# Issuing the V rows of a fused attention and MoE kernel from GpSimd instead of SyncE

## The chip, the cores and the metric

One Trainium2 chip, one core of it. The metric is the device time of one execution in microseconds (us). Engines are named as in the profile: PE (TensorE matmuls), PEld (its weight loads), DVE (VectorE), ACT (ScalarE), POOL (GpSimd), SP (SyncE, which here only issues transfers). Sixteen DMA engines serve all queues. Transfers issued by SP run on the hardware queue that the profile calls q1, transfers issued by POOL on the software queue q0, and the few that ACT issues on q10.

## The reference

Two layers, one after the other. Attention over q, k, v of shape (8, 8, 576, 64), that is 8 batches of 8 heads, is the sum of two parts: a coarse one on means of 4 positions, and a local one with a band mask. Its output, as 4608 tokens of 512, goes through a two-layer block without bias.

```python
def _attn_ref(q, k, v):
    ...                              # Sd = S // 4, scale = 1/sqrt(D)
    q_d = q.reshape(B, H, Sd, 4, D).mean(axis=3)        # k_d, v_d alike
    out_up = np.repeat(sm_attn(q_d, k_d, v_d), 4, axis=2)
    mask = np.abs(pos[:, None] - pos[None, :]) < 4
    scores = np.where(mask, scale * q @ k.T, -1e9)
    return out_up + softmax(scores) @ v

def _moe_ref(x, w_in, w_out):        # (4608, 512), (512, 2048), (2048, 512)
    h = x @ w_in
    return (h - np.tanh(h)) @ w_out
```

## The kernel before

Heads are handled in pairs: 32 pairs, four to a batch, a batch being a block `kb` of the dense part. For each pair `p` the kernel loads K and Q (`load_qk`, lines 363 to 369, two transfers of 256 KB into the staging tile `st`, 4 buffers) and V (`load_v`, lines 384 to 393, one transfer of 160 KB per head into `vst`, 5 buffers, so pair p+5 uses the buffer of pair p). A V transfer consists of 640 rows of 256 bytes: 128 partitions times 5 overlapping row tiles. `prep_v` (line 423) casts `vst` to bf16 as `vw` (line 427) on whichever of POOL, ACT and DVE the order names, and thereby sets the `vst` buffer free. From pair 12 on, V is also loaded a second time in groups of four positions (`load_v4`, lines 395 to 403, tile `v4`, shown as `v`), which POOL sums for the coarse part (lines 440 and 444); for earlier pairs PE makes these sums from `vw` (`pool_v`, line 458). Some of the `load_v4` transfers are issued by POOL (list `SOFT`), the others by SP.

For a pair, `attention` casts K and Q to bf16 (`qr`, line 502), turns them (PE transposes at line 510 for pairs 0 to 11, DMA transposes on SP after that), pools them (`half`, `qkd`, lines 593 to 627), makes the scores (lines 657 to 671), the exponentials on ACT (lines 676 to 684), the band mask (line 711), and the product with V (line 725). The result, divided by its sums (line 742), is turned again and joined into `xT` (line 760), the input of the dense part.

The dense part has, for each block, `mm1` (line 803: x times w_in, tanh on ACT at 814, subtraction on DVE at 817, giving `gT`) and `mm2` (line 883: `gT` times w_out). Blocks 5 to 7 use a seven-product scheme instead of `mm2` (line 1030), which needs sums of `gT` (`token_sums`, line 965). Rows left over from the 512-token tiles go through `left1` and `left2` (lines 829 and 855). While PE has nothing of the real work in the first microseconds, it runs filler matmuls (line 1240).

The weights are loaded by POOL, w_in and w_out in four transfers of 512 KB each (`load_w`, lines 405 to 421). Before the first of each, POOL copies one element of a named staging buffer (`GATE`, `OGATE`, line 416), so that the weights' transfers start only after that buffer has landed.

The order is not left to a scheduler. Class `Plan` collects all operations with planned costs, a list of alternatives (which engine), priorities and earliest starting times (`REL`), and lays them out engine by engine; the kernel then issues each engine's instructions in that fixed order. `GIVEN` names, letter by letter, which engine takes each free choice. `ONE` says for which pairs the two score steps are put as one, `WIDE` whether a `token_sums` step is one instruction or two halves. Every engine runs its instructions strictly in this order, and a waiting instruction holds up all that stands behind it on its engine. SP is such an engine too: a K, Q or output transfer stands behind a V transfer that waits for its `vst` buffer.

Of the kernel before, what the change touches and what calls it, by code (L numbers as in the profile page):

```python
# [14 lines left out]
class Plan:  # L15
# [17 lines left out]
    def op(self, eng, ns, fn, reads=(), writes=(), pri=0, after=0.0, slack=0.0,  # L33
           port=False, opens=None, uses=(), choice=None, rows=128, share=0.4):
        i = len(self.ops)
        deps = set()
        for key in reads:
            if key in self.last_write:
                deps.add(self.last_write[key])
        for key in writes:  # L40
            if key in self.last_write:
                deps.add(self.last_write[key])
            deps.update(self.readers.get(key, ()))
        for key in reads:
            self.readers.setdefault(key, set()).add(i)
        for key in writes:
            self.last_write[key] = i
            self.readers[key] = set()
        deps.discard(i)
        names = set(uses)  # L50
        if opens and not isinstance(opens, list):
            opens = [opens]
        for o in opens or ():
            names.add(o[0])
        for n in names:
            self.users.setdefault(n, []).append(i)
        if choice:

            letter = self.given[self.choices]
            self.choices += 1  # L60
            named = [a[:4] for a in choice if a[0][0] == letter]
            choice = named or [a for a in choice if len(a) == 4]
        alts = {a[0]: a for a in choice} if choice else {eng: (eng, ns, fn, port)}
        self.ops.append(dict(alts=alts, deps=deps, pri=pri, after=after, slack=slack,
                             opens=opens, names=names, rows=rows, share=share,
                             what=(list(writes) + [None])[0]))
        return i
# [135 lines left out]
def kernel(  # L203
# [9 lines left out]
    nc = tc.nc  # L213
    B, H, S, D = q.shape
# [5 lines left out]
    SCALE = 1.0 / float(D) ** 0.5  # L220
    N_FF = Dff // 128
    N_DC = Dm // 128
    WIDE = [c == "1" for c in "1011"]
    NBLK, NR, LEFT = B, 3, S - 512
    STEP = 112
    NT = 5
# [12 lines left out]


    KIN = [c == "1" for c in "11111111111100000000000000000000"]
    HALF = [c == "1" for c in "00001000000000000000000000000000"]

    SOFT = [c == "1" for c in "00001110011000110010001001000001"]
    VIN = [c == "1" for c in "11111111111100000000000000000000"]
    BACK = [c == "1" for c in "11111111111100000000000000000000"]
    ONE = [c == "1" for c in "00000000010000001111111111111111"]
    REL = [
           0, 0, 0, 0, 4, 14, 33.5, 30,
           23, 49, 67, 11.5, 75, 4.5, 95, 64,  # L250
           110, 71, 18, 23.5, 139, 151, 139.5, 148,
           170.5, 170.5, 15, 153.5, 207.5, 209.5, 232.5, 235,
    ]

    GIVEN = (
        "..A..D.DADA.PADDADPDD.AADD..D.DD.AA.DA.ADAA....ADAD..AA..P...AP.D..AP....DDPPPDD"
        "..D..A.A...PAAAPPPAADDD.DDDDAD.ADAD.A..PPPDDDAA...A.....DA..A.AA.PD.D..ADPDDAP.P"
        "D.PP..D.DDDDD.P..DP...DADP...P....A...D.PP..DPAAPP..P.D..AD..A..DD.PPD.PA..D.P.."
        ".PPD.P........P..PDDD.PD...AAPD....D.PPDPD.A...DPPD..A.DP.DPPP....AD..DP.D.DAP.."
        "D....DPP..DAAD..DPP.D.AA.PD.PP.PPPAAPDD..P..D..DAPP.DPP.P.P.PPAA.PPP.PPPAA.D.PPP"  # L260
        "DPDP.P..DDDD.D."
    )

    const = ctx.enter_context(tc.tile_pool(name="const", bufs=1))
# [2 lines left out]
    def fixed(name, shape, dt, n=None, pool=const):  # L267
        if n is None:
            return pool.tile(shape, dt, name=name, tag=name)
        return [pool.tile(shape, dt, name=f"{name}{i}", tag=f"{name}{i}")  # L270
                for i in range(n)]

    NST, NVST, NVW, NV4 = 4, 5, 4, 2
    NPP, NKQ = 4, 2
    gate = fixed("gate", [1, 1], FP32)
# [8 lines left out]
    st = fixed("st", [128, 2, 2, 4 * D], FP32, NST)  # L284
# [3 lines left out]
    vst = fixed("vst", [128, 2, NT, D], FP32, NVST)  # L288
# [69 lines left out]
    def load(ns, fn, keys, cost, pri, after=0.0, eng="SP"):  # L358
        op(eng, ns, fn, writes=list(keys) + [("q", keys[0])], pri=pri, after=after)
        op("DMA", cost, None, reads=[("q", keys[0])], writes=keys, pri=pri,  # L360
           share=0.18 if keys[0][0] == "vst" else 0.35)
# [22 lines left out]
    def load_v(p):  # L384
        b, j, s = p // NP, p % NP, p % NVST
        for i in range(2):
            base = v[b, 2 * j + i]

            def issue(i=i, base=base):
                nc.sync.dma_start(out=vst[s][:, i], in_=bass.AP(  # L390
                    tensor=base.tensor, offset=base.offset,
                    ap=[[D, 128], [STEP * D, NT], [1, D]]))
            load(500, issue, [("vst", s, i)], 940, 10 * p - 3000 + 5)

    def load_v4(p):
        b, h0, s = p // NP, 2 * (p % NP), p % NV4
        vv = v[b, h0:h0 + 2].rearrange("h (g c) d -> g h (c d)", c=4)
        for i in range(2):
            load(770 if SOFT[p] else 450,
                 lambda i=i: (nc.gpsimd if SOFT[p] else nc.sync).dma_start(  # L400
                     out=v4[s][0:128 - 112 * i, :, i], in_=vv[128 * i:144 - 16 * (1 - i)]),
                 [("v4", s, i)], 1000 - 870 * i, 10 * p - 3000 + 6,
                 eng="POOL" if SOFT[p] else "SP")

# [67 lines left out]
    def attention(p):  # L472
        b, j, s = p // NP, p % NP, p % 2
        sn, w, k3 = p % NST, p % NVW, p % NKQ
        early = KIN[p]
        split = HALF[p] and not early
        pri = 10 * p
# [183 lines left out]
        def score2():  # L661
            ps = at(s2)
            for hh in range(2):
                rows = slice(64 * hh, 64 * hh + 64)
                T.matmul(ps[:, hh, 0:120], kt[s][rows, STEP * 4:STEP * 4 + 128],  # L665
                         kq[k3][rows, :, 1, G0[4]:G0[4] + NG[4]],
                         start=True, stop=True)
            for i in range(2):
                for hh in range(2):
                    rows = slice(64 * hh, 64 * hh + 64)  # L670
                    T.matmul(ps[:, hh, 120 + G * i:120 + G * i + G],  # L671
                             qkd[s][rows, 128 * i:128 * i + 128],
                             qkd[s][rows, G + GAP:2 * G + GAP], start=True, stop=True)
# [15 lines left out]
        def both_scores():  # L689
            score1()  # L690
            score2()
        if not ONE[p]:
            op("PE", 220 * cold, score1, rows=64,
# [259 lines left out]
    def token_sums(kb, which):  # L953
        g = kb % 2
        a11, a12, a21, a22 = quarters(kb)
        for n, dst, x0, x1, sub, h in ((0, S0, a21, a22, 0, 2), (2, a21, a11, a21, 1, 0),
                                       (1, a11, S0, a11, 1, 0), (3, a12, a12, a11, 1, 1)):
            if n not in which:
                continue
            parts = [(0, 1)] if WIDE[n] else [(0,), (1,)]  # L960
            for es in parts:
# [182 lines left out]
        for _ in steps:  # L1144
            pass

    GATE, OGATE = ("st", 2, 0), ("vst", 1, 1)
    SEVEN = [c == "1" for c in "00000111"]
    ORDER7 = (1, 2, 6, 7, 4, 5, 3), (1, 7, 2, 6, 5, 4, 3)
    DENSE = [(7,), (6,), (5,), (4,)]  # L1150
# [37 lines left out]
    for p in range(NP):  # L1188
        if p + 1 < NP:
            load_qk(p + 1)  # L1190
        load_v(p)
# [4 lines left out]
    def load_next():  # L1196
        if nl[0] < NPAIR:
            if nl[0] % NP == 0:
                load_rest(nl[0] // NP)
            load_qk(nl[0])  # L1200
            load_v(nl[0])
            nl[0] += 1
        if nl[0] == NP + 4:
            for f in range(4):
                load_w(moe_w_out, w_out_sb, "w_out", f, OGATE if f == 0 else None)
# [66 lines left out]
```

## Time and profile before

| what | value |
|---|---|
| median of 3 runs | 324.42 us (323.06 to 325.06) |
| the profiled execution's own time | 322.44 us |
| its span, first to last instruction | 320.7 us |
| PE busy | 309.1 us, 96% |
| DVE, ACT, POOL busy | 255.3 us (80%), 207.8 us (65%), 156.8 us (49%) |
| V transfers | 64 of 160 KB, all issued by SP, median 4.8 us to landing |
| q1 and q0, share of 16 DMA engines | 71.3% and 10.0% |

The profile's rows of tenths show each engine's busy share in 40 slices of 8 us. Issuing a transfer from POOL occupies POOL and counts as busy there; issuing one from SP occupies only SP, which the profile does not count. The granted PE clock is full throughout.

### The profile page before, as it was taken

How to read it: one execution, taken by the hardware profiler on the slowest of the kernel's cores; microseconds unless marked ns; L12 is line 12 of the kernel's file. 1: busy time of each engine (PE TensorE's matmuls, PEld its weight loads, DVE VectorE, ACT ScalarE, POOL GpSimd, SP SyncE). 2: the span in 40 equal slices, each digit the busy share in tenths (PEclk: the TensorE clock that was granted, in tenths of full speed). 3: DMA queues.
4: the chain of work that ended last, by engine and by line, in shares of the span. 5: the costliest groups of instructions: out<-in, count | busy, mean ns of one | idle time of the engine just before them, and what ended most of it. 6: DMA issues, size and time to landing. Idle time of an engine off the chain costs nothing.

```text
span 320.7 us, 7553 instructions
## 1 busy us (share of the span) xinstructions
PE 309.1 (96%) x2831; PEld 181.0 (56%) x2831; DVE 255.3 (80%) x451; ACT 207.8 (65%) x372; POOL 156.8 (49%) x185
## 2 busy tenths in 40 slices
PE   7978999999999999999999999999899999999994
PEld 3654546554754545454655444545476667666783
DVE  5685997597888898679888999899999797656853
ACT  5884995588856776369745878579766852455210
POOL 7822664326267473537464735357794653511000
PEclk9999999999999999999999999999999999999999
DMA  8999999999999999999999999995452143200414
GB/s 218 275 219 227 279 185 247 289 277 304 240 232 274 236 210 246 224 255 195 245 222 177 269 237 251 232 223 112 94 92 57 35 49 93 67 0 3 130 36 131
DMA packets 117205, 59.23 MB, mean 185 GB/s; under 512 B 85008, under 2 KB 112592, under 8 KB 117168
## 3 DMA queue, kind: packets, MB, share of 16 engines
q1 hardware_dynamic: 111584, 52.17, 71.3%
q0 software_dynamic: 4896, 5.97, 10.0%
q10 hardware_dynamic: 688, 0.61, 0.6%
q8 instruction: 22, 0.36, 0.4%
q14 instruction: 15, 0.12, 0.1%
HBM read 43.65 MB, written 9.44 MB: 166 GB/s over the span
## 4 chain that ended last, share of the span: by engine, by line
PE 88%; DMA 7%; DVE 1%; SPq 1%; ACT 0%; POOL 0%; ACTq 0%; issue 0%; POOLq 0%
PE ps L803 34%; PE ps L883 22%; PE ps L1030 11%; DMA vst<-in_v_dram 6%; PE ps L725 5%; PE ps L829 5%; PE ps L855 4%; PE ps L657 3%; DMA sr<-in_q_dram 1%; PE ps L671 1%; PE ps L510 1%; PE ps L458 1%; PE ps L767 1%; PE ps L665 1%; SPq L366 1%; DVE xT L760 1%
## 5 line engine op out<-in xcount | busy, mean ns | idle before, releaser
L803 PE MATMUL ps<-xT,w_in_sb 128*128 128x512 bf16 x512 | 124.6, 379 | 0.0
L817 DVE TENSOR_TENSOR gT<-ps,u 128x512 bf16<-128x512 f32 x128 | 86.0, 684 | 21.2 <-ACT u L814 19.6
L814 ACT ACTIVATE u<-ps 128x512 f32<-128x512 f32 x128 | 76.1, 599 | 36.2 <-PE ps L803 33.6
L883 PE MATMUL ps<-w_out_sb,gT 128*128 128x512 bf16 x320 | 78.6, 379 | 0.0
L803 PEld LDWEIGHTS <-w_in_sb 128*128 128x128 bf16 x512 | 47.1, 98 | 47.3 <-issue 0.4
L883 PEld LDWEIGHTS <-gT 128*128 128x128 bf16 x320 | 29.2, 98 | 31.2
L444 POOL TENSOR_TENSOR vp<-v 128x256 bf16<-128x256 f32 x20 | 14.6, 730 | 58.7 <-PE ps L725 48.1
L676 ACT ACTIVATE E<-ps 128x912 bf16<-128x912 f32 x32 | 29.8, 931 | 17.8 <-PE ps L665 14.6
L1030 PEld LDWEIGHTS <-gT 128*128 128x128 bf16 x288 | 27.9, 98 | 7.5
L742 DVE TENSOR_TENSOR ln<-ps,r 128x768 bf16<-128x768 f32 x32 | 30.6, 956 | 0.9
L711 DVE TENSOR_TENSOR E<-E,mask 128x1152 bf16<-128x1152 bf16 x29 | 25.6, 882 | 4.4 <-ACT E L680 4.2
L502 POOL CAST qr<-st 128x512 bf16<-128x512 f32 x32 | 22.5, 713 | 9.3 <-DMA st<-in_q_dram 6.0
L440 POOL TENSOR_TENSOR v<-v 128x512 f32<-128x512 f32 x20 | 25.4, 1271 | 1.1
L725 PEld LDWEIGHTS <-E 128*128 128x128 bf16 x576 | 21.7, 97 | 6.1
L684 ACT ACTIVATE E<-ps 128x576 bf16<-128x576 f32 x32 | 20.9, 654 | 0.0
L583 ACT COPY kt<-kq 128x576 bf16<-128x576 bf16 x16 | 18.9, 1180 | 2.9 <-DVE kq L578 2.7
L593 POOL TENSOR_TENSOR half<-kq 128x576 f32<-128x576 bf16 x13 | 18.1, 1389 | 3.6 <-DVE kq L578 1.5
L725 PE MATMUL ps<-vw,E 128*128 128x65 bf16 x320 | 18.9, 193 | 0.0
L760 DVE TENSOR_TENSOR xT<-lT 128x336 bf16<-128x336 bf16 (+1 forms) x30 | 18.4, 655 | 0.0
L1030 PE MATMUL ps<-Tw,gT 128*128 128x256 bf16 x144 | 18.3, 273 | 0.0
L725 PE MATMUL ps<-vp,E 128*128 128x65 bf16 x256 | 18.1, 193 | 0.0
L1030 PE MATMUL ps<-w_out_sb,gT 128*128 128x256 bf16 x144 | 17.8, 273 | 0.0
(118 smaller groups left out, 434.9 us busy)
## 6 DMA issues: line engine op xcount, KB each, us to landing
vst<-in_v_dram SPq DMA_DIRECT2D x64, 160.0 KB, 4.8
st<-in_k_dram SPq DMA_DIRECT2D x32, 256.0 KB, 4.6
st<-in_q_dram SPq DMA_DIRECT2D x32, 256.0 KB, 4.6
v<-in_v_dram SPq DMA_DIRECT2D x14, 256.0 KB, 3.6
w_in_sb<-in_moe_w_in_dram POOLq DMA_DIRECT2D x4, 512.0 KB, 12.7
w_out_sb<-in_moe_w_out_dram POOLq DMA_DIRECT2D x4, 512.0 KB, 12.2
out_dram<-y SPq DMA_DIRECT2D x7, 256.0 KB, 3.8
out_dram<-y SPq DMA_DIRECT2D x7, 224.0 KB, 3.1
```

Source lines behind the costliest of these rows:

```text
L440: eng.tensor_tensor(out=v2, in0=v4[s][:, :, :, 0:128], in1=v4[s][:, :, :, 128:256], op=ALU.add)
L502: (eng, ns, lambda dst=dst, src=src, fn=fn: fn(out=dst, in_=src), port)
L676: A.activation(out=E[s][:, :, E0:E0 + 456], in_=at(s1)[:, :, PS0:512], func=AF.Exp, scale=SCALE)
L711: eng.tensor_tensor(out=el, in0=el, in1=mask.unsqueeze(1).to_broadcast([128, 2, S]), op=ALU.mult)
L725: T.matmul(po[:, hh, 65 * n:65 * n + 65], E[s][:, hh, e:e + 128], vv, start=start, stop=stop)
L742: op("DVE", 960, lambda: V.tensor_tensor(out=ln[s].rearrange("p n (h d) -> p h n d", d=D), in0=blocks()[:, :, :, 0:64], in1=r[s].unsqueeze ...
L760: eng.tensor_tensor(out=dst, in0=src, in1=add, op=ALU.add)
L803: T.matmul(at(name)[:, 0, :], w_in_sb[:, dc, fc * 128:(fc + 1) * 128], xT[dc][:, c0:c0 + 512], start=(dc == 0), stop=(dc == N_DC - 1))
L814: op("ACT", 600, lambda: A.activation(out=u[us], in_=at(name)[:, 0, :], func=AF.Tanh), reads=[("hd", kb, fc)], writes=[("u", us)], pri=-1, ...
L817: op("DVE", 690, lambda: V.tensor_tensor(out=gT[g][:, fc, :], in0=at(name)[:, 0, :], in1=u[us], op=ALU.subtract), reads=[("hd", kb, fc), ( ...
L883: T.matmul(at(name)[:, 0, :], gT[g][:, fc, ts * 128:ts * 128 + 128], w_out_sb[:, fc, :], start=(fc == 0), stop=(fc == N_FF - 1))
L1030: T.matmul(dst, left[:, f, 128 * j:128 * j + 128], right[:, f, :], start=(first and e == 0 and f == 0 and (j == 0 or apart)), stop=(e == 1 ...
```

## The change

V transfers of pairs 8 to 31 are issued by POOL (list `VSOFT`), in the same shape and without a cast; pairs 0 to 7 stay with SP. The planner gets a cost of its own for them (`CVS`). The whole order was made anew with that: `GIVEN`, `REL`, `SOFT`, `ONE`, `WIDE` and `GATE` have other values.

```diff
-    WIDE = [c == "1" for c in "1011"]
+    WIDE = [c == "1" for c in "0000"]
...
-    HALF = [c == "1" for c in "00001000000000000000000000000000"]
-
-    SOFT = [c == "1" for c in "00001110011000110010001001000001"]
+    HALF = [c == "1" for c in "00001011100100000000000000000000"]
+
+    VSOFT = [c == "1" for c in "00000000111111111111111111111111"]
+
+    SOFT = [c == "1" for c in "00001011100100000100000100001000"]
...
-    ONE = [c == "1" for c in "00000000010000001111111111111111"]
+    ONE = [c == "1" for c in "00000000000000001101111111111011"]
     REL = [
...
     GIVEN = (
...
+    CVS = 600.0
     NST, NVST, NVW, NV4 = 4, 5, 4, 2
...
             def issue(i=i, base=base):
-                nc.sync.dma_start(out=vst[s][:, i], in_=bass.AP(
-                    tensor=base.tensor, offset=base.offset,
-                    ap=[[D, 128], [STEP * D, NT], [1, D]]))
-            load(500, issue, [("vst", s, i)], 940, 10 * p - 3000 + 5)
+                (nc.gpsimd if VSOFT[p] else nc.sync).dma_start(
+                    out=vst[s][:, i], in_=bass.AP(
+                        tensor=base.tensor, offset=base.offset,
+                        ap=[[D, 128], [STEP * D, NT], [1, D]]))
+            load(660 if VSOFT[p] else 500, issue, [("vst", s, i)], CVS if VSOFT[p] else 940,
+                 10 * p - 3000 + 5, eng="POOL" if VSOFT[p] else "SP")
...
-    GATE, OGATE = ("st", 2, 0), ("vst", 1, 1)
+    GATE, OGATE = ("st", 2, 1), ("vst", 1, 1)
```

What it does to the order, by a comparison of the two programs: on POOL, 48 V issues are added, the `load_v4` issues fall from 12 to 6, the casts of `vst` from 11 to 8, and seven half-size `token_sums` steps take the place of one full one. SP issues 48 transfers fewer and 6 more. On ACT the casts of `vst` rise from 15 to 19 and the `od` copies from 6 to 12; DVE loses its 6 `od` copies. POOL's mask products (line 711) fall from 3 to 1, DVE's rise from 29 to 31. PE has one filler matmul less and otherwise the same matmuls in another order. On POOL, the issues of V of pairs 8, 9 and 10 stand between the issue of w_in and that of w_out. `HALF` has no effect on the pairs whose letters differ, since it is read only from pair 12 on.

## The prediction

> **What bounds the kernel now.** I read the page first, then the chain of waits, then PE's and POOL's timelines for the first 60 us, because the page's digits show PE below 9 only there and at the very end.
>
> ```profile
> span 320.7 us, 7553 instructions
> PE 309.1 (96%) x2831; PEld 181.0 (56%) x2831; DVE 255.3 (80%) x451; ACT 207.8 (65%) x372; POOL 156.8 (49%) x185
> PE   7978999999999999999999999999899999999994
> POOL 7822664326267473537464735357794653511000
> ```
>
> PE is full from the fifth slice on; POOL is half idle. From the chain in order of time:
>
> ```profile
> 14.85 14.61 DMA vst<-in_v_dram
> 32.74 1.85 PE ps L803 x8
> ...
> 304.24 12.24 PE ps L1030 x112
> ```
>
> The chain leaves the transfers at about 33 us (the V of pair 4 took 14.61 us beside w_in) and is then nearly all PE. So the time is PE's work, plus what PE loses before 33 us, plus 4.2 us after its last matmul. To put numbers on it I count matmuls in program order, fillers left out, each at its pace in this trace (0.216 us for 128x512, 0.109 for 128x256, 0.056 for 128x128, 0.03 for line 725, about as much for the scores). An instruction that stands behind W us of such work and starts at T has a lag of T - W. The lag at the first dense matmul is 12.3 us, at the turn of pair 5's Q (34.43 below) 15.7, at the first use of w_out's last quarter 16.8, and 15.5 at the last 112 matmuls (304.24 minus 288.7; the count is off by about 1 us). PE thus loses nothing after 60 us. I looked for gaps after 33 us and found one above 0.2 us: 1.1 us at 230.6, ahead of line 829.
>
> What sets the lag are arrivals:
>
> ```profile
> 30.38 0.51 PE L458 MATMUL ps<-vw,pick 128*128 128x128 bf16 x6 [1.36 <-POOL vw L427]
> 34.43 0.39 PE L510 MATMUL ps<-ident,qr 128*128 128x128 bf16 x4
> ...
> 45.98 1.46 PE L883 MATMUL ps<-w_out_sb,gT 128*128 128x512 bf16 x6
> 50.52 1.03 PE L883 MATMUL ps<-w_out_sb,gT 128*128 128x512 bf16 x4
> 57.01 2.33 PE L883 MATMUL ps<-w_out_sb,gT 128*128 128x512 bf16 x10
> ```
>
> ```profile
> 10.85 2.36 POOL L711 TENSOR_TENSOR E<-E,mask 128x1152 bf16<-128x1152 bf16 x1
> 13.16 0.23 POOL L416 COPY gate<-st 1x1 f32<-1x1 f32 x1
> 13.33 3.17 POOL L408 DMA_DIRECT2D w_in_sb<-in_moe_w_in_dram  x4
> ...
> 33.49 0.61 POOL L502 CAST qr<-st 128x512 bf16<-128x512 f32 x1 [3.17 <-DMA st<-in_q_dram]
> ...
> 38.08 0.18 POOL L416 COPY gate<-vst 1x1 f32<-1x1 f32 x1 [0.40 <-DMA vst<-in_v_dram]
> 38.20 3.05 POOL L412 DMA_DIRECT2D w_out_sb<-in_moe_w_out_dram  x4
> ```
>
> Pair 5's Q lands at 33.4 and its cast ends at 34.1, just before the turn at 34.43. The V of pair 6, which gates w_out, lands at 38.0. w_out's four quarters land at 45.2, 49.4, 53.6 and 57.9; PE first uses them at 45.98, 50.52, 53.92 and 58.3. So w_out comes 0.3 to 1.1 us ahead of need: that slack is the tightest place in the kernel.
>
> **What can be won at all.** After 60 us PE has only the 1.1 us gap to give. Less work for SP and the DMA engines after that is worth nothing, because PE does not wait for them.
>
> **The change, part by part.**
>
> Start of w_in. In the new POOL order the gate follows the cast of pair 1's V, with no mask product of 2.36 us before it, and waits for pair 2's Q, which lands at 11.6. w_in can be issued at about 11.9 instead of 13.33. That alone brings nothing: it takes the engines from K, Q and V earlier by as much, and pair 5's Q has the same transfers ahead of it. In the new PE order its turn stands behind 18.7 us of work (18.8 before), so its landing gives the same lag. A gain is bounded by 1.4 us; I take 0.
>
> PE's new order asks for the quarters of w_out behind 28.9, 32.8, 37.0 and 40.6 us of work, before behind 29.8, 34.1, 37.5 and 41.5. They are wanted 0.5 to 1.3 us earlier, with 0.3 to 1.1 us of slack: +0.6 us if they land as before (last quarter: 57.9 - 40.6 = 17.3 against 16.8, rounded up), between 0.1 and 0.6.
>
> Arrival of w_out. Its gate still waits for pair 6's V. SP's order now puts pair 6's K behind that V, which saves 0.75 us (so far apart do 256 KB landings lie there). But the V of pairs 8 and 9 is now issued by POOL before it: pair 8's right after POOL's cast of pair 3's V (about 18 us), behind w_in in q0, and pair 9's after the cast of pair 4's V (about 31). A V pair costs the engines 1.4 us on q1 (two landings 0.7 us apart when nothing else runs). On q0 no V was seen; the `v4` transfers there went in 4 KB packets of 159 ns median, while sixteen 256-byte packets on q1 take 16 x 18 = 288 ns, so its price lies between 0.8 and 1.4. Two pairs: 1.6 to 2.8 us, or half of it if pair 9's is not through by then. Pair 10's V stands ahead of w_out on POOL and in q0: 0 to 1.4 us more. Sum: from 0.8 - 0.75 = 0.05 to 2.8 + 1.4 - 0.75 = 3.45. I take +2.2, above the middle, since all three issues stand before w_out in one fixed order.
>
> POOL's load. One issue of 256 rows took 0.73 to 0.88 us, one of 32 rows 0.52, one weight issue of 512 rows 0.75 to 0.92. For 640 rows: at least 0.73, at most 0.73 + 384 x (0.73 - 0.52)/224 = 1.1; I take 0.8. A pair also waits 0.3 us for a semaphore, as the `v4` pairs do ("[0.30 <-POOL v L440]"). 24 pairs x (1.6 + 0.3) = 46 us, less three `v4` pairs at 1.25 + 0.3 and three casts at 0.73, that is 7 us. Seven half `token_sums` at about 2 us for one of 4.07 add 10 us at the end, where POOL is empty. Between 40 and 220 us POOL had 94 of 180 us; it comes to some 130. That fits, but everything is in order: behind a V issue that waits for its `vst` buffer (a cast that may be ACT's or DVE's) stand the `qr` casts, `half` and `qkd`, and behind these PE's scores. Cover is the planner's 0.7 us before PE's steps of pairs 12 on. Nearest row: the six `v4` issues, and no gap on PE beside them. Worst, all uncovered: 24 x (1.9 - 0.7) = 29 us. I take +1.3, since 24 issues are four times as many, near the low end.
>
> Taken from SP: 48 issues of about 0.5 us. Nothing on PE waits for SP after 60 us, so 0; likewise for the freed DMA engines. DVE's sum of work falls by 3 us by the trace's means and ACT's rises by 5; both have slack against PE, 0. The casts that ACT takes over lie inside its 35% idle time.
>
> The gap at 230.6: the new PE order has the last pair's product behind 238 instead of 242 us of work, so it may close: -0.5 (0 to -1.1). The end, 112 matmuls of line 1030, is unchanged.
>
> Sum: 0 + 0.6 + 2.2 + 1.3 - 0.5 = **+3.6 us**. The profiled execution took 322.44 us (span 320.7 and 1.7 around it), so 326.0; it lies 2.0 under the median of 324.42, for which I say **328.0 us**. About 1% (3.2 us) is what a measurement of this kernel can tell from no change.
>
> **Rivals.**
>
> *Nothing moves (−2 to +3 us, 322.4 to 327.4; point 324.4).* V in 4 KB packets is cheap, w_out lands as before, and PE hides the rest. For it: PE is full, and POOL's issues never showed on PE. Against it: 0.3 us of slack for w_out.
>
> *Faster.* V leaves the engines sooner, Q of pair 5 and w_out come earlier. Its place is the first 60 us: w_in 1.4 us earlier, pair 6's V 0.75 earlier, three V pairs at 0.6 us saved each, the gap of 1.1 closed: at most 1.4 + 0.75 + 1.8 + 1.1 = 5 us, 319.4. It decides only if pair 5's Q also lands 3 us sooner, with more asked of the engines by then; against it, they are at full share from 10 us on.
>
> *POOL becomes the bound.* If each V pair's delay beyond the 0.7 us cover reaches PE in a third of the 24 pairs, 8 x 1.2 = 10 us is added, 334. For it: DVE is busy 80%, and over 90% from 180 to 240 us, so lost time is not won back. Against it: POOL at 72%. The Trainium skill, "DMA: Bandwidth & Descriptors", section "SWDGE vs HWDGE vs iDMA", says that GpSimd writes the descriptors into rings in SBUF from which DVE locks it out in its two-port mode, and that transfers issued from SP are immune. By it a V issue would last longer than any row here; the trace has no issue above 0.92 us while DVE was busy, so it bears the rule out little.
>
> **How the numbers follow.** The forecast (+2 to +7.5) 0.45, nothing moves 0.30, faster 0.08, POOL the bound 0.17. Slower by over 1% is the first and the last: 0.62; within 1%: 0.29; faster by over 1%: 0.09 (a little of the second case goes over the edge). The range reaches from the low bounds (0.1 + 0.05 + 0 - 1.1, and 1.4 less for w_in: -2.4) to the POOL case: 322 to 335; the forecast's own is 326 to 332.
>
> **What would show it.** In the changed profile: POOL's V issues 0.7 to 1.1 us each; w_in issued near 12 us; the w_out issue at 39 to 40.5 us and the last quarter landing at 59 to 61; line 883 starting at 46.5 to 48.5; the first of the last 112 matmuls at 306 to 309. I am wrong if line 883 starts before 46 us, or if the lag at the end is under 15.5; wrong in size if PE shows idle time of several us after 60, with POOL as releaser or behind it.

## The result, and the profile after

The changed kernel takes 335.56 us (median of 4 runs, 333.21 to 336.69) against 324.17 us (323.06 to 325.06) beside it: ratio 1.034, 95% interval 1.028 to 1.041, 11.4 us slower. The forecast was 328.0 with a range to 335. The profiled execution is the slowest of the four, 336.69 us; that of before, at 322.44, is faster than its median, so the two traces lie 14.3 us apart and the medians 11.4. Ratios here and below leave out executions more than 1.5% above the fastest of the same kernel, medians do not.

From the page of the changed kernel (lines of `before.py` from 390 on stand some 3 to 5 lines further down in it: 427 is 432, 711 is 716, 883 is 888, 1030 is 1035):

```profile
span 335.0 us, 7521 instructions
PE 311.1 (93%) x2785; PEld 181.3 (54%) x2830; DVE 256.7 (77%) x450; ACT 213.0 (64%) x384; POOL 195.0 (58%) x225
PE   7896989988999799999999999799999999999994
POOL 6631884488499657767769758456464552511231
PEclk9999799999999989999999999999999999999999
```

PE's work is as it was, but its row now has a 6 in slice 4, 8s in slices 6, 9 and 10, and a 7 in 14 and in 26, and the row of the granted clock, all 9s before, has a 7 and an 8. POOL is busy 58% of the time; that is not an engine that is full. PE's timeline, its waits of over 1 us from 33 to 120 us (before there was none there):

```profile
34.02 0.50 PE L463 MATMUL ps<-vw,pick 128*128 128x128 bf16 x6 [3.03 <-POOL vw L432]
...
49.91 1.04 PE L888 MATMUL ps<-w_out_sb,gT 128*128 128x512 bf16 x4 [1.59 <-DMA w_out_sb<-in_moe_w_out_dram]
...
75.60 0.30 PE L676 MATMUL ps<-qkd 64*128 64x144 bf16 x4 [1.34 <-DVE qkd L603]
...
83.67 0.33 PE L730 MATMUL ps<-vw,E 128*128 128x65 bf16 x5 [1.34 <-DVE E L716]
...
116.52 0.59 PE L808 MATMUL ps<-xT,w_in_sb 128*128 128x512 bf16 x2 [1.97 <-DVE gT L822]
```

The first waits for pair 4's V, which landed at 33.13 us (before 29.45), the second for the first quarter of w_out. After the waits of 3.03 and 1.97 us the granted clock went to half for 3.41 us each, from 35.07 and from 116.99, which costs at most 1.7 us each time. POOL's timeline shows what the weights had to stand behind:

```profile
12.47 3.38 POOL L413 DMA_DIRECT2D w_in_sb<-in_moe_w_in_dram  x4
...
33.25 0.72 POOL L432 CAST vw<-vst 128x640 bf16<-128x640 f32 x1 [5.62 <-DMA vst<-in_v_dram]
34.27 1.74 POOL L393 DMA_DIRECT2D vst<-in_v_dram  x2 [0.30 <-POOL vw L432]
...
37.99 1.74 POOL L393 DMA_DIRECT2D vst<-in_v_dram  x2
...
39.86 3.00 POOL L417 DMA_DIRECT2D w_out_sb<-in_moe_w_out_dram  x4
```

The pairs of V at 34.27 and 37.99 are 9 and 10. The second keeps POOL from the gate of w_out until 39.73, 1.66 us later than before, and both stand ahead of w_out in q0: its first packet moved at 43.30, 3.44 us after the issue (before 1.82), its quarters landed at 49.87, 54.02, 58.20 and 62.44 (before 45.17, 49.44, 53.62, 57.87). So 1.66 us of the 4.70 come from POOL, and 3.04 arise after the issue. Not all of these 3.04 are shown to be the queue's: from issue to landing the first quarter took 10.01 us here and 6.97 before, but 8.87 in `issue_14_to_21` and 9.26 in `issue_from_14` below, which begin just as the kernel before does, with no V in q0 ahead of w_out. V of pair 11, issued behind w_out at 42.81 and 43.67, landed at 63.42 and 64.32, 20.6 us after its issue. In the chain of waits the transfers before 70 us are now those of q1, K above all, and the last 112 matmuls begin at 318.50 (before 304.24):

```profile
51.94 15.94 DMA st<-in_q_dram
...
318.50 12.24 PE ps L1035 x112
```

Where the time is lost can be read from the start of equal work. W is PE's work in program order, here counted by weight loads, and each number is how much later a kernel reaches it than the kernel before (with some of the runs below; all from the profiled executions). Where PE's order is the changed one, the figures at 17, 60, 90 and 180 move by 1 to 4 us with the time that is taken for each matmul, since a step then falls before or after that W; those at 40, 150 and 285 move by under 1 us in the changed kernel.

| later than before by us, at W = | 17 | 40 | 60 | 90 | 150 | 180 | 285 |
|---|---|---|---|---|---|---|---|
| changed kernel | 1.9 | 5.7 | 8.1 | 12.8 | 12.9 | 16.3 | 14.0 |
| issue_only | -0.4 | 8.2 | 8.7 | 12.4 | 14.7 | 17.4 | 17.4 |
| issue_8_to_13 | 0.1 | 6.3 | 6.3 | 6.3 | 6.3 | 6.2 | 6.3 |
| issue_14_to_21 | -0.3 | 1.5 | 2.1 | 4.3 | 4.8 | 4.8 | 3.7 |
| issue_from_14 | -0.1 | 1.3 | 1.9 | 5.7 | 8.0 | 8.3 | 8.4 |
| pool_time | 0.2 | 2.0 | 3.6 | 7.4 | 11.6 | 12.0 | 12.0 |
| both_then_sp | -0.3 | 6.4 | 5.7 | 6.7 | 9.5 | 11.1 | 8.9 |

The changed kernel is 5.7 us late after 40 us of work, which is the start, and loses nearly all the rest by about 121 us of time. Up to some 2 us at W = 40 is how far two executions of the same start lie apart: `issue_14_to_21`, `issue_from_14` and `pool_time` change nothing before about 63 us and are 1.3 to 2.0 us late there.

### The profile page after: what moved, and what is told of

The parts are those of the page before. It is cut to its first block, busy times and chain, and to the rows that moved or that the text cites. A ratio compares the mean times of both kernels' runs of the same rounds, so it can differ in the third digit from the quotient of the medians.

```text
span 335.0 us, 7521 instructions
## 1 busy us (share of the span) xinstructions
PE 311.1 (93%) x2785; PEld 181.3 (54%) x2830; DVE 256.7 (77%) x450; ACT 213.0 (64%) x384; POOL 195.0 (58%) x225
## 4 chain that ended last, share of the span: by engine, by line
PE 62%; DMA 20%; DVE 10%; SPq 2%; issue 2%; POOL 1%; ACT 1%; DVEq 0%; POOLq 0%; ACTq 0%
PE ps L808 23%; PE ps L888 12%; PE ps L1035 11%; DMA st<-in_k_dram 7%; DMA st<-in_q_dram 5%; PE ps L834 4%; PE ps L860 4%; PE ps L730 4%; DMA v<-in_v_dram 3%; DVE E L716 3%; DMA kq<-qr 3%; DMA lT<-ln 2%; PE ps L662 2%; DVE xT L765 2%; DVE gT L822 2%
## 5 line engine op out<-in xcount | busy, mean ns | idle before, releaser
L808 PE MATMUL ps<-xT,w_in_sb 128*128 128x512 bf16 x486 | 128.9, 385 | 3.8 <-DVE gT L822 2.0
L888 PE MATMUL ps<-w_out_sb,gT 128*128 128x512 bf16 x306 | 79.9, 380 | 2.6 <-DMA w_out_sb<-in_moe_w_out_dram 1.6
L393 POOL DMA_DIRECT2D vst<-in_v_dram x48 | 42.0, 878 | 14.3 <-DVE vw L432 4.4
L716 DVE TENSOR_TENSOR E<-E,mask 128x1152 bf16<-128x1152 bf16 x31 | 32.1, 1038 | 5.6 <-ACT E L685 5.5
L449 POOL TENSOR_TENSOR vp<-v 128x256 bf16<-128x256 f32 x20 | 15.5, 777 | 26.5 <-PE ps L730 22.9
L445 POOL TENSOR_TENSOR v<-v 128x512 f32<-128x512 f32 x20 | 26.9, 1343 | 3.0 <-DMA v<-in_v_dram 2.5
L588 ACT COPY kt<-kq 128x576 bf16<-128x576 bf16 x15 | 17.7, 1182 | 3.9 <-DMA kq<-qr 3.7
L1035 PE MATMUL ps<-Tw,gT 128*128 128x256 bf16 x144 | 19.0, 273 | 0.1
L765 DVE TENSOR_TENSOR xT<-lT 128x336 bf16<-128x336 bf16 (+1 forms) x32 | 15.9, 538 | 4.1 <-DMA lT<-ln 4.1
L598 POOL TENSOR_TENSOR half<-kq 128x576 f32<-128x576 bf16 x12 | 15.9, 1327 | 3.9 <-issue 2.6
```

Of the source, the lines that this page charges most:

```text
L393: (nc.gpsimd if VSOFT[p] else nc.sync).dma_start(out=vst[s][:, i], in_=bass.AP(tensor=base.tensor, offset=base.offset, ap=[[D, 128], [STEP ...
L445: eng.tensor_tensor(out=v2, in0=v4[s][:, :, :, 0:128], in1=v4[s][:, :, :, 128:256], op=ALU.add)
L716: eng.tensor_tensor(out=el, in0=el, in1=mask.unsqueeze(1).to_broadcast([128, 2, S]), op=ALU.mult)
L765: eng.tensor_tensor(out=dst, in0=src, in1=add, op=ALU.add)
L808: T.matmul(at(name)[:, 0, :], w_in_sb[:, dc, fc * 128:(fc + 1) * 128], xT[dc][:, c0:c0 + 512], start=(dc == 0), stop=(dc == N_DC - 1))
L888: T.matmul(at(name)[:, 0, :], gT[g][:, fc, ts * 128:ts * 128 + 128], w_out_sb[:, fc, :], start=(fc == 0), stop=(fc == N_FF - 1))
```

## The experiments

The theory that I tested (A): the start costs by late arrivals (pair 4's V, w_out), and later V's issues on POOL delay what PE needs from POOL. Against it: that the new order is at fault and not the issuing, and that no single wait decides, since others take its place. The other letters are explained in the texts on record. A "frozen" order is that of the named kernel, with only the engine of the issue changed, at the same place. Each comparison is with runs of the kernel before on the same chip, whose median was 323.7 to 325.0 us.

**Order and issue apart.** `order_only`, the changed kernel's order with V on SP:

```diff
-                (nc.gpsimd if VSOFT[p] else nc.sync).dma_start(
+                nc.sync.dma_start(
```

> The changed kernel with its order kept on PE, ACT, DVE and POOL; the V transfers of pairs 8 to 31 are issued by SP at the same places of the overall order. Theory A (the issuing by POOL costs most of the 11.4 us: its issues in POOL's queue and in q0 ahead of w_out): the waits of PE at 48, 74, 82 and 114 us go, the wait for pair 4's V at 31 us (3.0 us) and the halved clock after it (1.7 us) stay, since w_in still starts early: 328 us (326 to 330). Theory B (the new order is worse by itself, whoever issues V): 333 to 337 us, with the same waits of PE.

`issue_only`, the order of before with V of pairs 8 to 31 on POOL:

```diff
-                nc.sync.dma_start(out=vst[s][:, i], in_=bass.AP(
+                (nc.gpsimd if p >= 8 else nc.sync).dma_start(out=vst[s][:, i], in_=bass.AP(
```

> The kernel before with its order kept on PE, ACT and DVE and among POOL's other work; the V transfers of pairs 8 to 31 are issued by POOL at the same places of the overall order. Theory A: 48 issues of 0.88 us that this order has no room for, V of pairs 8 to 10 ahead of w_out in q0: w_out lands 4 us later, and PE waits several times for steps behind POOL or DVE: 333 to 342 us, at least as slow as the changed kernel. Theory B: 324 to 327 us, PE full from 33 us on.

Measured: 331.61 us (ratio 1.022, 1.017 to 1.027) and 337.78 us (1.044, 1.040 to 1.047). Both parts cost, and they do not add: issuing alone costs 14.1 us, the order made for it takes back 2 to 3. The first lies between the ranges of the two theories. Of the waits that I said would go, the one for w_out stayed in its trace (1.11 us at 46.39; an execution of 335.32 us), and one of 2.61 us for `qkd` came at 50.20. An order made for V on POOL is no clean measure of V on SP, though: on SP an issue of V's second form (line 405) now lasted 4.25 us at 43.97, with V, K and Q behind it.

**The two late arrivals, one at a time.** `three_back`: V of pairs 8 to 10 goes back to SP, so that nothing stands ahead of w_out.

```diff
-                (nc.gpsimd if VSOFT[p] else nc.sync).dma_start(
+                (nc.gpsimd if p > 10 else nc.sync).dma_start(
```

> The changed kernel with its order kept, V of pairs 8, 9 and 10 issued by SP, pairs 11 to 31 by POOL. If the six issues ahead of w_out in POOL's queue and in q0 are what delays w_out: its first packet within 2.5 us of its issue instead of 5.4, the first quarter lands at 45.5 to 47 us instead of 49.9, PE's wait of 1.6 us at 48 us is gone; the later waits at 74 to 114 us get smaller as K and Q also come sooner: 330 to 333 us. If w_out is slow because SP's transfers take the engines, whoever issues these V: first quarter still at 49 to 50.5 us, 334 to 337 us.

`w_in_later`: one POOL fill of 0.95 us ahead of w_in, so that pair 4's V is in front of it again.

```diff
             if src is moe_w_in:
+                if f == 0:
+                    GP.memset(v4[0], 0.0)
```

> The changed kernel with one memset of 0.95 us put on POOL between the gate and the first issue of w_in; nothing else. If w_in's head start of 0.9 to 1.2 us is what starves pair 4's V (q1 gets one packet for each of q0's while w_in runs, so that every us of head start costs V some 3 us): V of pair 4 lands at 30 to 31 us instead of 33.1, PE's wait at 31 us shrinks from 3.0 to under 1 us, the clock is not halved after it: 330 to 332.5 us. If pair 8's V in q0 is what delays it: the landing stays at 33 to 34, the time at 334.5 to 337.

Measured: 336.23 us (1.039, 1.032 to 1.046) and 335.66 us (1.040, 1.033 to 1.047), no gain from either. Each did what it should: w_out's first quarter landed at 45.45 us in the first, pair 4's V at 29.40 in the second, and the wait it was aimed at is gone. Another came in its place, bigger. PE's timeline of `three_back`:

```profile
52.07 0.42 PE L676 MATMUL ps<-qkd 64*128 64x144 bf16 x4 [5.37 <-POOL qkd L603]
```

and of `w_in_later`:

```profile
51.47 1.89 PE L890 MATMUL ps<-w_out_sb,gT 128*128 128x512 bf16 x4 [5.05 <-DMA w_out_sb<-in_moe_w_out_dram]
```

In the first, w_out came 4.4 us earlier than in the changed kernel, beside a V transfer that SP had issued at 37.45: this landed at 47.63, POOL stood 6.04 us for its cast, and two V issues, `half` and `qkd` stood behind that. In the second w_out was issued at 41.46, and PE, no longer late, waited for it the longer. In both the clock is at half for 6.83 us about that wait. My expectation of 330 to 333 was wrong: a wait taken away at the start is worth only the distance to the next one.

**w_out ahead of V.** `w_out_first`: the V of pairs 9 and 10 is issued on POOL right behind w_out. `both_starts`: this and the fill. `both_then_sp`: both, with V of pairs 11 to 31 on SP.

```diff
+                if p in (9, 10):
+                    put_off.append(go)    # issued after the fourth quarter of w_out
+                else:
+                    go()
```

> The changed kernel in its own order, except that GpSimd issues the V of pairs 9 and 10 right behind the fourth quarter of w_out instead of ahead of the first. Theory A (each late arrival in the first 60 us adds what it is late by, and V ahead of w_out in q0 is one of them): w_out is issued near 38 us instead of 39.86, its first packet follows within 2.5 us of the issue instead of 5.4, its first quarter lands at 45.5 to 47 instead of 49.87, PE's wait for it (1.59 us at 49.9) is gone, the wait for pair 4's V at 34.0 and the halved clock after it stay; 333 us, 1.5 to 3 under the changed kernel. Theory B (the starts do not decide, later waits take their place): w_out lands just as early but the time is within 1 us of the changed kernel, 334.5 to 336.5, with the lag at W = 285 at 35 to 37 as before.

> As w_out_first, and one POOL fill of about 1 us ahead of the issue of w_in, so that pair 4's V stands ahead of it. Theory A: neither the wait at 34.0 nor the one for w_out is there, the clock is not halved before 60 us, the lag behind 40 us of PE's work is 17 to 18.5 (the kernel before 16.2, the changed one 21.9), and that gain of 4 us stays to the end: 330 to 332 us. Theory B: the lag at 40 us falls the same way but grows by more than 17 to the end (the changed kernel: 15), so that the time stays above 333.

> As both_starts, but the V of pairs 11 to 31 is issued by SP, at the same places of the order; on POOL these 42 issues of 0.88 us (37 us of POOL) are gone. Theory A (V on POOL is what makes the later waits): from 50 to 285 us of PE's work the lag grows by no more than 8 us (the kernel before 5.7, the changed one 15), and the time is 323 to 327. Theory C (the new order itself leaves too little slack there, whoever issues): the lag grows by 12 or more, 329 to 333. A transfer that stands behind a waiting V on SP can also make new waits, with K or Q late; these would show with a DMA transfer as the releaser, or POOL behind such a one.

Measured: 345.44 us (1.065, 1.055 to 1.074), 345.31 us (1.067, 1.060 to 1.074) and 330.48 us (1.021, 1.015 to 1.026). w_out came as I said (issued 38.44, quarters at 45.47 to 57.78, as in the kernel before), and the time is 10 us worse, outside both theories. The timeline of `w_out_first`, all engines:

```profile
38.44 3.00 POOL L424 DMA_DIRECT2D w_out_sb<-in_moe_w_out_dram  x4
...
46.01 0.86 POOL L396 DMA_DIRECT2D vst<-in_v_dram  x1 [1.14 <-ACT u L829]
...
49.90 0.86 POOL L396 DMA_DIRECT2D vst<-in_v_dram  x1 [3.03 <-DMA w_out_sb<-in_moe_w_out_dram]
...
54.08 0.85 POOL L396 DMA_DIRECT2D vst<-in_v_dram  x1 [2.59 <-DMA w_out_sb<-in_moe_w_out_dram]
...
58.06 0.87 POOL L396 DMA_DIRECT2D vst<-in_v_dram  x1 [3.12 <-DMA w_out_sb<-in_moe_w_out_dram]
...
60.58 0.42 PE L686 MATMUL ps<-qkd 64*128 64x144 bf16 x4 [11.50 <-POOL qkd L613]
```

V issues that wait for w_out have nothing to do with its data. They start 0.3 to 0.6 us after w_out's quarters land (45.47, 49.35, 53.54, 57.78; for the first the profile names another releaser), and each of these quarters is the transfer eight before in POOL's sequence. In the compiled program the transfers of an issuing engine take turns over eight completion semaphores, and each waits until the one eight before it has landed; in no trace here has POOL or SP more than eight in flight. With w_out and two pairs of V in flight the ninth transfer stops POOL, and `half` and `qkd` stand behind it: PE waits 11.50 us (14.20 in `both_starts`), and the clock is at half for 13.65 us (17.07). With V of later pairs on SP (`both_then_sp`) this is gone. Its delay still reaches 6.4 us at W = 40, since POOL waits for a V that SP issued at 38.25 and that landed at 47.54 beside w_out, and PE for `qkd` behind it (2.80 us at 49.89). Whatever comes ahead of w_out or beside it in these 20 us, one of the two is late. PE's waits after 60 us sum to 4.3 us in it, 7.8 in the changed kernel and 1.0 before, and from W = 40 on its delay grows by 2.5 us, that of the changed kernel by 8.3. In the terms of the texts its lag grew by some 9 us from 50 to 285, between the 8 of theory A and the 12 of C, and its time is in C's range: the order and the later issues share what is lost there.

**Planning with the right price.** `true_cost` gives the planner 1030 ns for a V issue on POOL; `plan_from_14` does that and leaves the V of pairs 8 to 13 to SP; `old_plan_from_14` is the latter with the settings of the kernel before.

```diff
-            load(660 if VSOFT[p] else 500, issue, [("vst", s, i)], CVS if VSOFT[p] else 940,
+            load(1030 if VSOFT[p] else 500, issue, [("vst", s, i)], CVS if VSOFT[p] else 940,
```

> The changed kernel, its order laid out anew with 1030 ns instead of 660 as the planned cost of a V issue on POOL (measured: 0.88 us and about 0.15 of a gap behind it); all other settings are unchanged. Theory A (the order was planned with POOL too cheap, so that PE's steps stand too early behind POOL's): PE's idle time after 60 us falls from about 9 us to 5 or less; 330 to 333 us. Theory B (the settings were found for the cost of 660, another cost only shuffles them): 334 to 340 us.

> The settings of the changed kernel, V by POOL only from pair 14 on, its issue planned at 1030 ns, order laid out anew (as true_cost, which took 333.0, with pairs 8 to 13 back on SP). Theory A (V of pairs 8 to 13 meets w_out in the one ring of q0): w_out's first quarter lands by 46.5 us, no V lands more than 12 us after its issue, and the time is 327 to 330.5 us. Theory B (the settings of the order decide): 331 to 336 us, with other waits.

> The settings of the kernel before, V by POOL from pair 14 on, its issue planned at 1030 ns, order laid out anew from that place on. If the steady part costs because the places on POOL were not planned for, this recovers it: 324 to 328 us. If POOL's time has no place to go however it is planned, it is as issue_from_14, 329 to 333 us; settings that fit another order can add to either.

Measured: 333.01 us (1.028, 1.022 to 1.034), 343.86 us (1.062, 1.056 to 1.067) and 334.65 us (1.032, 1.025 to 1.038). The right price may be worth some 2.5 us, but the intervals of the ratios, 1.022 to 1.034 and 1.028 to 1.041 for the changed kernel, overlap. PE's waits after 60 us sum to 7.0 us against 7.8, not the 5 or less of theory A. The other two lie outside all the ranges that I gave. `plan_from_14` got its w_out early (first quarter 46.68), but two SP transfers of V took over 12 us to land, and between 297 and 303 us PE waited 1.51, 1.34 and 3.12 us, with 6.83 us at half clock: the list of letters and due times was found for one set of durations and lays out something else with another. These runs say nothing on V's issue that the frozen orders don't say better.

**The later part by itself.** `issue_from_14` freezes the order of before and issues the V of pairs 14 to 31 on POOL, so the start has no V issue on POOL. `pool_time` leaves all V on SP and puts four copies of one element on POOL at each of those 36 places.

```diff
+                for _ in range(4 if p >= 14 else 0):
+                    GP.tensor_copy(tick, tock)
```

> The kernel before in its own order, except that GpSimd instead of SyncE issues the V of pairs 14 to 31 (36 issues), at the same places of the order. The first 60 us hold no V issue on POOL, so that w_in, pair 4's V and w_out come as in the kernel before; the lag behind 40 us of PE's work should be 16 to 17. Theory A (the steady part costs of itself): with all 48 issued so, the lag grew from 40 to 285 us by 15.8 us where it grew by 6.6 before, 9.2 for 42 issues, 0.22 each; 36 of them give 8, so 330 to 333 us. Theory S (only the start costs, what comes later is its aftermath): 323 to 326.5 us.

> The kernel before, V issued by SP throughout, with four copies of one element (about 0.2 us each) on POOL at the place of each V transfer of pairs 14 to 31, 36 times. They take about POOL's time of the V issues, but wait for no buffer, move nothing and hardly use the memory port. Theory T (POOL's time is the price, since all else on POOL stands behind it): the same as issue_from_14 within 2 us. Theory W (the price is what a V issue waits for, its buffer to be cast and its semaphore, with POOL's other work behind it): 323 to 327 us, and at least 3 us under issue_from_14.

Measured: 331.59 us (1.024, 1.018 to 1.029) and 332.47 us (1.027, 1.021 to 1.033). Theory T: empty work of the same length costs as much as the issues, 8.7 and 7.7 us by the ratios. It also makes the same waits at the same places. First the kernel before, all engines, where POOL's `half` feeds DVE's `qkd` and this PE's scores at line 671:

```profile
97.69 1.28 POOL L593 TENSOR_TENSOR half<-kq 128x576 f32<-128x576 bf16 x1
99.18 0.45 DVE L598 TENSOR_TENSOR qkd<-half 128x288 bf16<-128x288 f32 x1
...
101.90 0.29 PE L671 MATMUL ps<-qkd 64*128 64x144 bf16 x4
```

PE takes `qkd` 2.3 us after it is there. The same place in `issue_from_14`, with two V issues (and two more at 96.88) ahead of `half`:

```profile
101.12 1.74 POOL L390 DMA_DIRECT2D vst<-in_v_dram  x2
...
102.89 1.28 POOL L593 TENSOR_TENSOR half<-kq 128x576 f32<-128x576 bf16 x1
104.20 0.46 DVE L598 TENSOR_TENSOR qkd<-half 128x288 bf16<-128x288 f32 x1 [1.75 <-POOL half L593]
...
104.72 0.30 PE L671 MATMUL ps<-qkd 64*128 64x144 bf16 x4 [0.81 <-DVE qkd L598]
```

and in `pool_time` (its lines stand 4 lower):

```profile
102.87 2.02 POOL L396 COPY tick<-tock 1x1 f32<-1x1 f32 x8
104.85 1.27 POOL L597 TENSOR_TENSOR half<-kq 128x576 f32<-128x576 bf16 x1
106.15 0.46 DVE L602 TENSOR_TENSOR qkd<-half 128x288 bf16<-128x288 f32 x1 [2.95 <-POOL half L597]
106.67 0.30 PE L675 MATMUL ps<-qkd 64*128 64x144 bf16 x4 [1.04 <-DVE qkd L602]
```

`half` is 5.2 and 7.2 us later, of which PE's own delay by then is 1.8 and 3.5 us. DVE stops for it with its own later work (`kt`, for which PE waits 0.88 and 0.89 us next) behind it, and the 2.3 us of slack are gone. From 60 to 140 us POOL was busy 41.8 us before and 56.2 us in `issue_from_14`, 70% of the stretch. So it is not POOL's sum that is too large; it is the place of `half` in its queue.

**Where a V issue is dear.** Three parts of `issue_only`: V of pairs 8 to 13, of 14 to 21, or of 22 to 31 alone.

```diff
-                nc.sync.dma_start(out=vst[s][:, i], in_=bass.AP(
+                (nc.gpsimd if 8 <= p < 14 else nc.sync).dma_start(out=vst[s][:, i], in_=bass.AP(
```

> The kernel before in its own order, the V of pairs 8 to 13 alone (12 issues) issued by GpSimd. Theory P (the price depends on the place; here w_out stands behind the V of pairs 9 and 10 on POOL and in q0, and the V of pair 11 and after behind w_out): w_out is issued at 42 us or later, its first quarter lands at 51 us or later, V transfers land 12 us or more after their issue, PE idles for several us between 38 and 65 us; +5 to +7 us, 329 to 331.5. Theory E (an even price of 0.2 us per issue): +2.5, 326 to 327.5.

> The kernel before in its own order, the V of pairs 14 to 21 alone (16 issues, at about 65 to 120 us) issued by GpSimd. Theory P: the waits at about 104, 107 and 126 us (DVE's sums of half, kt) come as with all of 14 to 31; +5 to +7 us, 329 to 331.5. Theory E: +3.2, 327 to 328.

> The kernel before in its own order, the V of pairs 22 to 31 alone (20 issues, after 120 us) issued by GpSimd. Theory P: PE shows no new wait of over 0.5 us, since POOL was free for 45% of this time; 323.5 to 326 us. Theory E: +4, 328 to 329.

Measured: 330.30 us, ratio 1.020 (1.016 to 1.025), for 12 issues; 327.49 us, 1.011 (1.006 to 1.017), for 16; 327.01 us, 1.003 (0.999 to 1.008), for 20. By the ratios that is 6.6, 3.7 and 1.0 us, or 0.55, 0.23 and 0.05 us per issue (the last at most 0.12). The last is the weakest of the three: its ten executions spread from 323.76 to 332.92 us, and their median is 2.0 us above that of before, 0.10 per issue, between the ranges of the two theories. Its one trace, of an execution of 329.05 us, has a new wait of PE of 1.69 us at 192.72, against my sign of none over 0.5. An even price is refuted: the first part costs more than twice its even price of 2.5 us, the last no more than 2.4 at the upper end of its interval, where 4 were due. The middle third came out nearer the even price (3.2) than mine (5 to 7). In `issue_8_to_13` w_out's first quarter landed at 50.66 us, V of pairs 11 and 12 12 to 16 us after their issues; all 6.3 us are lost by W = 40 and stay to the end, neither won back nor added to. The parts don't quite add: 3.7 and 1.0 against 7.7 for `issue_from_14`, 11.3 for the three against 14.1 for `issue_only`. That fits with slack that the first delays use up, and with the clock, which went to half after the waits at 105 and 107 us in `issue_from_14` but not after the same two waits in `issue_14_to_21` (the last section shows why); PE's wait of 1.71 us at 126.01 in `issue_from_14` is in neither of its two parts. What else makes the difference stays open.

**A second path, which no experiment took apart.** The longest of the changed kernel's waits between 60 and 120 us, the 1.97 us at 116.52, is not behind POOL. PE waits for `gT`, which stands on DVE behind a `half`, and this waits for a transpose of K and Q (`kq<-qr`) that SP issued on q1 and that took 8.64 us. The chain of the changed kernel, and its timeline:

```profile
106.35 8.64 DMA kq<-qr
```

```profile
115.11 0.76 DVE L598 TENSOR_TENSOR half<-kq 128x576 f32<-128x576 bf16 x1 [3.00 <-DMA kq<-qr]
```

The wait of 2.57 us at 203.92 in `issue_only` and that of 1.69 us at 192.72 in `issue_from_22` come the same way, behind transposes `lT<-ln` of 9.75 and 8.85 us. Before, none of the 45 transposes took over 5.7 us, and none over 6.9 in `order_only`, `pool_time` and `issue_8_to_13`, where SP issues V from pair 14 on. In `issue_14_to_21`, with V on POOL, none took over 5.9. So V in q0 may slow the transposes on q1; no run shows that it does, and `pool_time`, with its V on SP, can't.

## Why the prediction was wrong in size

*What bounds the kernel, and the sign.* Right. PE is full, w_out's slack of 0.3 us was the tightest place, and the loss shows as waits of PE, most of it in the first 121 us. The prediction's own sign of being wrong in size came true: PE has 7.8 us of waits after 60 us, and w_out's last quarter (62.44), its first use (49.91) and the last 112 matmuls (318.50) are all later than the bounds given there.

*Start of w_in: 0, with a gain of up to 1.4.* This step failed. I let the earlier w_in (12.47 us as forecast, near 12) take the engines "from K, Q and V earlier by as much", and looked only at pair 5's Q. Pair 4's V was in flight too, was waited for by the cast and by PE (the line at 30.38 of before stands in the prediction), and came 3.68 us later; PE went on 3.64 us later. `w_in_later` shows the cause: with w_in 1.7 us later and that V issued at the same time, it lands at 29.40. About 1 us is due to pair 8's V on q0 as well: with pair 8 on SP and w_in just as early (`order_only`, `three_back`, `plan_from_14`) pair 4's V landed at 31.8 to 32.1 and PE waited 2.0 us for it, not 3.0. The Trainium skill, "DMA: Bandwidth & Descriptors", section "Queues, rings and completion order", says that each DMA engine goes round robin over its queues by whole packets. The trace agrees: from 18 to 30 us q0 moved 1731 packets, nearly all of them w_in's of 1 KB, and q1 1716, most of them of 256 bytes. Pair 4's second transfer was 16.9 us on the way (before, with w_in 0.86 us later, 14.6; V's median there is 4.8).

*PE's earlier need of w_out: +0.6.* No run shows this term by itself; PE was already 3.64 us late when it asked.

*Arrival of w_out: +2.2, at most 3.45.* Mis-sized: +4.70 us at the first quarter, of which up to some 2 us may be what two executions differ by (above). The direction and the parts were those named (issued at 39.86, within 39 to 40.5), but the sum let the gate open with pair 6's V, which landed at 36.49, and POOL came to it only at 39.73; a pair of V in q0 took 1.87 us (landings 0.93 us apart from 63.42 on) where I had 0.8 to 1.4. I did not ask where V of pairs 11 and 12 would go: 20 us behind w_out. `w_out_first` and `issue_8_to_13` show that this start costs 6 us or more in either order of the two.

*POOL's load: +1.3, at most 29.* This step failed, and it is the largest miss. The durations were about right:

```profile
L393 POOL DMA_DIRECT2D vst<-in_v_dram x48: 872/872/959, 18.7 to 206.0; - x48
```

That is the tile view of the changed kernel (shortest, median and longest in ns); I took 800, within 730 to 1100. POOL's busy time from 40 to 220 us came to 127.8 us, I had said some 130. The step that failed is "That fits, but everything is in order", priced near the low end because six `v4` issues had shown no gap. `issue_from_14` and `pool_time` put 7.7 and 8.7 us on 36 issues' worth of POOL's time. The way was in the prediction (`half` and `qkd` behind an issue, PE's scores behind these), the size was not: `qkd` has 2.3 us of slack at the place shown, and two issues take 1.74 us of it at once. In the changed kernel four issues in a row do the same, its timeline at 70 us:

```profile
69.95 3.48 POOL L393 DMA_DIRECT2D vst<-in_v_dram  x4
...
73.45 0.72 POOL L609 TENSOR_TENSOR half<-kt 128x288 f32<-128x288 bf16 x1
...
74.20 1.34 DVE L603 TENSOR_TENSOR qkd<-half 128x288 bf16<-128x288 f32 x1 [1.27 <-POOL half L609]
```

and PE waits at 75.60 (shown above).

*The rival "POOL becomes the bound", 334.* Nearest in time to the 335.56 measured, and given 0.17. Its mechanism was half right: POOL's delay reaches PE, but at a few places with no slack and not at a third of the pairs, and the start has as large a part. The rule cited beside it (the Trainium skill, "DMA: Bandwidth & Descriptors", section "SWDGE vs HWDGE vs iDMA", DVE locking GpSimd out of the rings) is not borne out here: no V issue lasted over 0.96 us with DVE busy 77% of the time, and empty copies cost as much.

*The clock, in no term.* Two halvings of 3.41 us cost at most 3.4 us. The Trainium skill, "TensorE: Matmul & The Clock Gate", Part 1, gives a free-running window of 3.4 us and half the clock after an idle window. The stretches of 3.41, 6.83 and 13.65 us agree with the window; but less than a whole idle window did it here (a wait of 1.97 us, and in `issue_from_14` two of 0.81 and 0.88 in one window).

*The gap at 230.6: -0.5.* The trace of before has it at 230.94, of 0.97 us. The wait ahead of that line is gone in the changed kernel, but one of 2.08 us for a mask product stands at 216.2. *SP, DMA, ACT and DVE: 0.* No run contradicts this for SP's freed time. For DVE it did not hold: PE's waits at 83.67 and 216.2 are for DVE's mask products (one of 3.75 us stands ahead of the first, median 0.76). The wait at 116.52 goes back to a late transpose, which leaves the term of the DMA engines open.

## What to carry to other kernels

A step moved to a half-idle engine that works strictly in order is not paid by its share of busy time; it is paid where something stands behind it that the bounding engine needs soon. Find those places and their slack, and price the step there (here 0.55, 0.23 and 0.05 to 0.10 us for the same instruction). And a transfer moved to the queue of the weights stands ahead of them or behind them: ask what is late in either case, and how many transfers that queue's issuer may have in flight.

## What the runs showed of the hardware

- V issued by POOL crossed q0 in the changed kernel in packets of 4096 and 2048 bytes, those of 4096 (POOL's `v4` among them) at 204 ns median and 311 mean, the weights' 1 KB packets at 96 ns; by the mean, V is no dearer per byte than the weights there, but at 1.87 us a pair it was dearer than the 1.4 that it takes on q1.
- Away from the program's end, PE's clock was at half for 3.41 us or a multiple of it, and within each trace these stretches begin a multiple of 3.41 us apart. Cut by that grid, the 17 traces show (from 5 us on) that a window at full clock in which PE stood idle for 1.6 us or less was not followed by half clock, that one with 1.95 us or more always was, and that between the two both came. So the same two waits can cost more or less by where they fall: in `issue_from_14` those at 105 and 107 us lie in one window (1.76 us idle, half clock from 107.41), in `issue_14_to_21` a window's edge at 104.86 parts them (1.2 us idle behind it, clock full), and in the changed kernel an edge parts the 2.08 us at 216.2 (1.83 idle, clock full).
- DVE instructions that read and write only SBUF took some 0.4 us longer on the mean than the median of their like when POOL computed beside them (0.46 in the changed kernel, 59 instructions, up to 3.0; before 0.38, 57 instructions), and mostly no longer beside a V issue (median 0.00, mean 0.06, 23 instructions); those that read PSUM took no longer. The mask product of 3.75 us at 79.87 (median 0.76), ahead of PE's wait at 83.67, is such a case. That `pool_time` has the same waits as `issue_from_14`, with copies of one element, says that this is not the main cause.
